# RWKV-6 attention and a SiLU feed-forward block: the recurrent state kept as its diagonal blocks, 48 columns per pair of heads instead of 128

## The chip, the cores and the metric

The kernel runs on one core of a Trainium2 chip. The time is device microseconds of that core, the median of several runs. A profile is one further execution, taken by the hardware profiler; its span runs from the first to the last instruction, and its own time is a little longer than the span.

The engines are named as in the profile: PE is the matrix engine (TensorE), PEld its weight loads, DVE the vector engine, ACT the scalar engine, POOL the GpSimd engine, SP the engine that issues most transfers.

## The reference

Inputs are r, k, v, w of shape (4 batches, 8 heads, 768 tokens, 48), u of shape (8, 48), and two weights of 384x2048 and 2048x384, all float32. Each head of each batch has a 48x48 state:

```python
for t in range(S):
    cur = np.einsum('bhd,bhe->bhde', u[None] * kt, vt)
    y[:, :, t] = np.einsum('bhd,bhde->bhe', rt, state + cur)
    state = wt[:, :, :, None] * state + np.einsum('bhd,bhe->bhde', kt, vt)
x = y.transpose(0, 2, 1, 3).reshape(B * S, H * D)
h = x @ w_in
out = (h * (1.0 / (1.0 + np.exp(-h)))) @ w_out
```

A row of the state belongs to one channel d of the key; the decay w scales a row as a whole.

## The kernel before

**Units.** Time is cut into 6 chunks of 128 tokens, and a unit is one chunk for two batches, so there are 12 units (0 to 11). Inside a unit the decay between tokens is built up in seven levels of doubling distance (`product`, `grow_keys`, `grow_queries`, `score_products`), which fill a 128x128 score per head. `y_state` multiplies the queries with the state of the chunks before (line 844), `y_values` multiplies scores with values (line 865) into the same PSUM banks, and `update` carries the state on. The feed-forward block runs two units behind: `up` (line 1001, then SiLU on ACT, line 1010), and `quarter` (line 1067), which forms the second product by seven products of half size in the manner of Strassen. `sums` makes the sums of activations that these need (DVE, line 1049). The results of the seven products go through two PSUM buffers called `p_o`; `quarter` drains each of them with an addition on DVE (line 1076), or with a copy on ACT for the first (line 1074). A product can start only when the one two places earlier has been drained.

**Pairs of heads.** Two heads share a tile: the even head has partitions 0 to 47, the odd one partitions 64 to 111 (PD = 64, D = 48, NP = 4 pairs). The state has a tile `[128, B, NP, 2 * PD]`, 2048 numbers in each partition. The head e of a pair uses rows 64e to 64e+47 and the columns of the same numbers: a diagonal block. The rest is zero from a memset (line 404) at the start.

**The update of the state** (from line 886). For each of the two batches, PE multiplies keys and values into a PSUM bank `p_kv`, 48 columns for each pair. POOL then multiplies the whole of the batch's state with the decay over the chunk (line 898; not for the units of the first chunk). After the second batch, DVE adds `p_kv` to the diagonal block, one instruction for the even heads and one for the odd heads (line 907). In units 0 and 1 it is a copy, on ACT and on DVE (line 909). Units 10 and 11 have no update, since nothing comes after them.

**The order of the work** is written out by hand: `mix(i)` returns the groups of unit i, and the steps of the feed-forward block are put between them. Each engine runs its own queue in that order. Around the update the order is `turn_apart`, `turn_k`, `y_state(i)`, `y_values(i)`, the transposes of the next unit's w and k on DVE (line 374) with the first `product` on POOL (line 422), a part of `sums`, then `update(i)`. Behind it POOL has `grow_own` (line 654), the other products (line 422) and `grow_own` once more. Unit 2's update stands a little apart: it is followed by unit 3's transposes, the products (line 422) and the start of the keys (line 669). DVE has the additions of `sums`, the addition to the state, the transposes of r (line 374) and `grow_queries` (line 627), and then the first drain of `quarter` (line 1076). `block_bonus` (POOL, line 507) and `block_sum` (DVE, line 541) compute the terms of near tokens.

Of the kernel before, what the change touches and what calls it, by code (L numbers as in the profile page):

```python
# [8 lines left out]
F32 = mybir.dt.float32  # L9
# [29 lines left out]
def kernel(  # L39
# [11 lines left out]
    nc = tc.nc  # L51

    B, H, S, D = r.shape
    DM, DF = moe_w_in.shape
    L = 128
    NL = 7
    NB = 2
    NP = H // 2
    PD = 64
# [14 lines left out]
    const = ctx.enter_context(tc.tile_pool(name="const", bufs=1))  # L74
# [9 lines left out]
    def bank(name, *dims):  # L84

        have = banks[name][turns_of[name] % 2][:]
        turns_of[name] += 1
        steps, n = [], 1
        for d in dims[::-1]:
            steps.insert(0, [n, d])  # L90
            n *= d
        return bass.AP(tensor=have.tensor, offset=have.offset, ap=[have.ap[0], *steps])
# [193 lines left out]
    make_identity(nc, ident)  # L286


    state = const.tile([128, B, NP, 2 * PD], F32, name="state")

    room = pt.tile([128, 4, DM // 2], F32, name="partial", bufs=1).rearrange("p x d -> p (x d)")
    spread = room[:, 0:4 * L].rearrange("p (s b t) -> p s b t", s=2, b=NB)
# [65 lines left out]
    tw, tr, tk, diag, kq, xt = {}, {}, {}, {}, {}, {}  # L358
# [473 lines left out]
    def values(i, b):  # L832
        return vq[i] if b == 1 else vt[i]

    def y_state(i):

        n, b0 = units[i]
        for e in range(2):
            p_yt[i, e] = bank("p_m", NP, L)
        for p in range(NP):  # L840
            for b in range(NB):
                for e in range(2):
                    rows = slice(PD * e, PD * e + D)
                    nc.tensor.matmul(y_place(i, e, p, b), lhsT=state[rows, b0 + b, p, rows],  # L844
                                     rhs=tr[i][rows, b * NP + p, :], start=(p < 2 and b == 0), stop=False)

        half = L // 2
        for p in range(NP):
            for b in range(NB):
                rows, at = slice(b * half, (b + 1) * half), (2 * p + b) * D  # L850
                nc.tensor.matmul(y_place(i, b, p, b)[:, 0:half], lhsT=whole[i][b][rows, at:at + D],
                                 rhs=score[rows, i % NSC, b, b * NP + p, 0:half], start=False, stop=False)

    def y_place(i, e, p, b):

        x = p % 2
        return p_yt[i, e][PD * x:PD * x + D, p // 2 * NB + b, :]
# [27 lines left out]
    def update(i, b):  # L885
        n, b0 = units[i]
        if n == S // L - 1:
            return
        if b == 0:
            p_kv[i] = bank("p_m" if i < NTOK else "p_sc", NB, NP, D)  # L890
        for p in range(NP):
            for e in range(2):
                nc.tensor.matmul(p_kv[i][PD * e:PD * e + D, b, p, :], lhsT=kq[i, b][:, p, PD * e:PD * e + D],
                                 rhs=values(i, b)[:, 2 * p + e, :], start=(b == 0 and p == 0),
                                 stop=(b == NB - 1 and p == NP - 1))
        new = state[:, b0 + b]
        if n > 0:
            nc.gpsimd.tensor_tensor(out=new, in0=new,
                                    in1=tw[i][NL][:, b * NP:(b + 1) * NP, :].to_broadcast([128, NP, 2 * PD]),
                                    op=ALU.mult)  # L900
        if b < NB - 1:
            return
        for e in range(2):
            rows, cols = slice(PD * e, PD * e + D), slice(PD * e, PD * e + D)
            new = state[rows, b0:b0 + NB, :, cols]
            if n > 0:
                nc.vector.tensor_tensor(out=new, in0=p_kv[i][rows], in1=new, op=ALU.add)
            else:
                (nc.scalar.copy if i == 0 else nc.vector.tensor_copy)(out=new, in_=p_kv[i][rows])
# [29 lines left out]
    def mix(i):  # L939
# [15 lines left out]
        def start(j):  # L955
            return [*[(product, j, l) for l in range(1, NL)], (grow_own, j, 1)]

        end = [[*at(ahead, *bonus_steps(i + 1, 0, 1, 2, 3))],
               [*at(i < len(units) - NB, (turn_apart, i), (turn_k, i)), (y_state, i), *both(y_values, i), *at(ahead, *turns(i + 1)),
                (sums, i - 1, FH // 2 - 2), *both(update, i), *at(not ahead, (move_x, i))]]  # L960
        if i < NPAIR:
            groups = [[*both(turn, i, "w"), (product, i, 0)],
# [154 lines left out]
    for l in range(1, NL):  # L1117
# [9 lines left out]


    others = {1: [(bonus_sum, 1, 0), (bonus_sum, 1, 1), (load_rk, 2), *blocks[8:12]], 2: [*both(update, 0)],
              3: [(bonus_spread, 1), (reverse_v, 1), (clear, 1), (load_values, 2)]}  # L1130

# [4 lines left out]
    for m in range(1, 4):  # L1136
# [4 lines left out]
    do((scores, 1, NL - 1), (bonus, 2, 0), (bonus, 2, 1), (join_weight, 8), (add_weight,), (bonus_sum, 2, 0), (bonus, 2, 2), (up, 0, 7), *both(y, 1), (turn_apart, 1),  # L1141
       (tail_weight, 9), (turn_k, 1), (dense_x, 1, 0), (head_weight, 9, [0]), (dense_x, 1, 1), (head_weight, 9, [1]),
       (join_weight, 9), (add_weight,), (tail_weight, 10), (head_weight, 10), *both(update, 1), (bonus_sum, 2, 1), (load_rk, 3), (up, 1, 0), *both(turn, 2, "w"))
    blocks = block_loads(3)

# [5 lines left out]
    for m in range(6):  # L1151
# [8 lines left out]
    do((burst, 2, 5), (keep_level, 2, 5), (keep_level, 2, 6), (go_on, 2, 6), (bonus_write, 2), (up, 1, 6), (weight_sums, 1),  # L1160
       (load_values, 3), (turn_apart, 2), (turn_k, 2), (up, 1, 7), (weight_sums, 2), (sums, 1, 2))
    do((sums, 1, 3), (y_state, 2), *both(y_values, 2), *both(update, 2),
       (move_x, 2),
       *blocks[7:])
# [44 lines left out]
```

## Time and profile before

| what | value |
|---|---|
| median of 3 runs | 600.91 us (600.6 to 602.53) |
| time of the profiled execution | 601.18 us |
| its span | 599.4 us |
| PE busy | 590.6 us, 99% of the span |
| PEld busy | 529.7 us, 88% |
| DVE busy | 417.5 us, 70% |
| POOL busy | 361.3 us, 60% |
| ACT busy | 232.8 us, 39% |
| decay of the state on POOL (line 898) | 16 instructions, 20.7 us |
| memset of the state on POOL (line 404) | 1 instruction, 1.8 us |
| addition to the state on DVE (line 907) | 16 instructions, 8.8 us |
| products with the state on PE (line 844) | 320 matmuls, 48x48 weights, 128 columns |

The shares are means over the whole span. Matmuls overlap, and their ends are modelled, so an idle time of PE that the profile shows is less than the time that the array lost: the spacing of the starts of matmuls is the surer measure. An engine that waits for another is told with the one whose event came last.

### The profile page before, as it was taken

The numbers are of one execution on the slowest core, as the hardware profiler recorded it, in microseconds if no ns is written. First come the engines' busy times: TensorE is split into PE (matmuls) and PEld (weight loads), VectorE is DVE, ScalarE is ACT, GpSimd is POOL, SyncE is SP. The second block draws the span as 40 slices with busy tenths as digits, with TensorE's granted clock in tenths as the row PEclk, the third lists the DMA queues.
The fourth block names the chain that finished last, engine by engine and source line by source line (L and its number), as shares of the span: only waits on it lengthen the run. The fifth ranks groups of instructions, "written<-read, shape, count | busy, mean of one in ns | idle before, by whom it ended". The sixth has DMA issues, their size and how long they took to land.

```text
span 599.4 us, 15465 instructions
## 1 busy us (share of the span) xinstructions
PE 590.6 (99%) x6142; PEld 529.7 (88%) x6142; DVE 417.5 (70%) x709; ACT 232.8 (39%) x516; POOL 361.3 (60%) x414
## 2 busy tenths in 40 slices
PE   8999999999999999999999999999999999999997
PEld 7787876799899899899899889889889889889997
DVE  7879788798696695696696696687588587542041
ACT  6788884431530530540350351361351251250110
POOL 6998778357678568278578478577567567500000
PEclk9999999999999999999999999999999999999999
DMA  9966794342542543642643643643543531101000
GB/s 225 306 143 176 165 277 49 54 80 48 129 61 62 108 68 54 134 63 52 137 63 54 134 61 53 135 61 53 112 77 52 121 57 27 36 2 28 27 1 26
DMA packets 203080, 53.45 MB, mean 89 GB/s; under 512 B 186752, under 2 KB 194816, under 8 KB 203008
## 3 DMA queue, kind: packets, MB, share of 16 engines
q1 hardware_dynamic: 201424, 51.88, 42.3%
q8 instruction: 48, 0.79, 0.6%
q10 hardware_dynamic: 1584, 0.59, 0.5%
q14 instruction: 24, 0.20, 0.1%
HBM read 43.21 MB, written 5.24 MB: 81 GB/s over the span
## 4 chain that ended last, share of the span: by engine, by line
PE 74%; DVE 9%; POOL 4%; DMA 4%; ACT 3%; issue 3%; SPq 3%; DVEq 0%; POOLq 0%; ACTq 0%
PE p_h L1001 31%; PE p_o L1067 31%; PE p_m L1023 3%; PE p_sc L704 2%; PE p_m L865 2%; DVE temps L1049 2%; SPq L123 1%; PE p_m L844 1%; PE p_m L704 1%; DVE score L722 1%; POOL w_in_sb L255 1%; DMA tokens_w<-in_w_dram 1%; POOL tk L645 1%; DVE p_w L242 1%; DMA raw<-in_r_dram 1%
## 5 line engine op out<-in xcount | busy, mean ns | idle before, releaser
L1001 PE MATMUL p_h<-xt,w_in_sb 128*128 128x256 f32 x1152 | 259.5, 382 | 0.8 <-POOL tk L669 0.7
L1001 PEld LDWEIGHTS p_h<-xt,w_in_sb 128*128 128x128 f32 x1152 | 215.6, 190 | 32.1 <-POOL tk L669 0.9
L1010 ACT ACTIVATE gt<-p_h 128x512 f32<-128x512 f32 x90 | 53.5, 596 | 175.4 <-PE p_h L1001 175.1
L645 POOL TENSOR_TENSOR tk<-tk,tw 128x256 f32<-128x256 f32 x128 | 94.6, 759 | 32.9 <-issue 20.8
L1067 PE MATMUL p_o<-own,temps 128*128 128x192 f32 x528 | 88.7, 327 | 0.7 <-DVE temps L1076 0.7
L1067 PEld LDWEIGHTS p_o<-own,temps 128*128 128x128 f32 x528 | 86.0, 190 | 1.6 <-DVE temps L1076 1.6
L507 POOL TENSOR_TENSOR ruk<-tokens_rk 128x768 f32<-128x768 f32 (+1 forms) x32 | 50.6, 1594 | 60.8 <-DMA tokens_rk<-in_k_dram 36.9
L1067 PE MATMUL p_o<-w_out_sb,gt 128*128 128x192 f32 x508 | 86.6, 327 | 0.0
L1067 PEld LDWEIGHTS p_o<-w_out_sb,gt 128*128 128x128 f32 x508 | 83.3, 190 | 1.0 <-DVE partial L1076 0.4
L1049 DVE TENSOR_TENSOR temps<-gt 128x256 f32<-128x256 f32 x84 | 54.9, 653 | 25.5 <-ACT gt L1010 25.3
L627 DVE TENSOR_TENSOR tr<-tr,tw 128x512 f32<-128x512 f32 x61 | 54.8, 899 | 18.3 <-PE p_m L704 14.6
L422 POOL TENSOR_TENSOR tw<-tw 128x256 f32<-128x256 f32 (+6 forms) x83 | 41.0, 494 | 35.8 <-DVE tw L374 31.9
L615 ACT COPY tk<-tk 128x256 f32<-128x256 f32 x52 | 21.0, 403 | 105.2 <-POOL tk L645 77.6
L1049 DVE TENSOR_TENSOR temps<-temps,gt 128x256 f32<-128x256 f32 x43 | 32.6, 759 | 1.5
L722 DVE COPY_PREDICATED score<-mask,p_sc 128x512 f32<-128x512 int8 x42 | 31.2, 799 | 3.5 <-PE p_sc L704 3.3
L1067 PE MATMUL p_o<-w_out_sb,temps 128*128 128x192 f32 x176 | 30.4, 326 | 0.0
L541 DVE TENSOR_REDUCE block_sums<-ruk 128x4 f32<-128x192 f32 (+1 forms) x48 | 24.2, 546 | 7.1 <-POOL ruk L507 7.1
L1067 PEld LDWEIGHTS p_o<-w_out_sb,temps 128*128 128x128 f32 x176 | 28.9, 190 | 0.0
L1076 DVE TENSOR_TENSOR partial<-p_o,partial 128x192 f32<-128x192 f32 x33 | 11.7, 354 | 24.6 <-PE p_o L1067 24.6
L1076 DVE TENSOR_TENSOR temps<-p_o,partial 128x192 f32<-128x192 f32 x22 | 7.9, 358 | 29.8 <-PE p_o L1067 23.5
L870 ACT COPY yt<-p_m 48x512 f32<-48x512 f32 x40 | 23.2, 580 | 13.8 <-PE p_m L865 13.1
L704 PEld LDWEIGHTS p_sc<-tr,tk 48*32 48x32 f32 (+1 forms) x1312 | 18.2, 119 | 11.1 <-issue 8.1
(188 smaller groups left out, 821.9 us busy)
## 6 DMA issues: line engine op xcount, KB each, us to landing
w_out_sb<-in_moe_w_in_dram SPq DMA_DIRECT2D x6, 768.0 KB, 7.5
w_out_sb<-in_moe_w_out_dram SPq DMA_DIRECT2D x4, 768.0 KB, 5.6
own<-in_moe_w_out_dram SPq DMA_DIRECT2D x4, 768.0 KB, 6.4
tokens_rk<-in_r_dram SPq DMA_DIRECT2D x8, 384.0 KB, 4.5
tokens_rk<-in_k_dram SPq DMA_DIRECT2D x8, 384.0 KB, 5.5
tokens_w<-in_w_dram SPq DMA_DIRECT2D x8, 384.0 KB, 6.6
xt<-yt SPq DMA_DIRECT2D x60, 48.0 KB, 2.0
raw<-in_w_dram SPq DMA_DIRECT2D x80, 32.0 KB, 2.0
```

The source lines that it names most:

```text
L422: engine.tensor_tensor(out=up, in0=t[:, :, 0::2], in1=t[:, :, 1::2], op=ALU.mult)
L507: mul = lambda out, one, two: nc.gpsimd.tensor_tensor(out=out, in0=one, in1=two, op=ALU.mult)
L541: add = lambda out, have: nc.vector.tensor_reduce(out=out, in_=have, axis=mybir.AxisListType.X, op=ALU.add)
L627: nc.vector.tensor_tensor(out=odd, in0=odd, in1=tw[i][l][:, :, 0::2][:, :, :, None].to_broadcast([128, Q, L >> (l + 1), c]), op=ALU.mult)
L645: nc.gpsimd.tensor_tensor(out=out, in0=have, in1=odd_products(i, l, b, *blocks), op=ALU.mult)
L704: nc.tensor.matmul(to, lhsT=tk[i][rows, X[l % 2] + p, x * m:(x + 1) * m], rhs=have, start=True, stop=True)
L722: nc.vector.copy_predicated(out=dst, mask=masks[l][:, :, None].to_broadcast([128, NB, NP, ni, c]), data=sc[e].rearrange("p (b q) (i c) -> ...
L870: nc.scalar.copy(out=yt[i][PD * e:PD * e + D, x::2, :, :], in_=p_yt[i, e][PD * x:PD * x + D].rearrange("p (q b) t -> p q b t", b=NB))
L1001: nc.tensor.matmul(p_h[:, a, :], lhsT=w_in_sb[:, c, f * 128:(f + 1) * 128], rhs=xt[i][:, c, :], start=(c == 0), stop=(c == KC - 1))
L1010: nc.scalar.activation(out=gt[i, m], in_=p_h, func=AF.Silu)
L1049: nc.vector.tensor_tensor(out=out, in0=one, in1=two, op=op)
L1067: nc.tensor.matmul(p, lhsT=left(f), rhs=right[:, f, :], start=(f == 0), stop=(f == FH - 1))
```

## The change

The state becomes a tile of 48 columns for each pair of heads. The even head's block and the odd head's block lie in the same columns, on different partitions. The tile has 768 numbers in each partition instead of 2048.

```diff
-    state = const.tile([128, B, NP, 2 * PD], F32, name="state")
+    state = const.tile([128, B, NP, D], F32, name="state")
...
-                    nc.tensor.matmul(y_place(i, e, p, b), lhsT=state[rows, b0 + b, p, rows],
+                    nc.tensor.matmul(y_place(i, e, p, b), lhsT=state[rows, b0 + b, p, :],
                                      rhs=tr[i][rows, b * NP + p, :], start=(p < 2 and b == 0), stop=False)
...
             nc.gpsimd.tensor_tensor(out=new, in0=new,
-                                    in1=tw[i][NL][:, b * NP:(b + 1) * NP, :].to_broadcast([128, NP, 2 * PD]),
+                                    in1=tw[i][NL][:, b * NP:(b + 1) * NP, :].to_broadcast([128, NP, D]),
                                     op=ALU.mult)
...
         for e in range(2):
-            rows, cols = slice(PD * e, PD * e + D), slice(PD * e, PD * e + D)
-            new = state[rows, b0:b0 + NB, :, cols]
+            rows = slice(PD * e, PD * e + D)
+            new = state[rows, b0:b0 + NB]
```

The order of the instructions on every engine and what each waits for stay as they were. The memset on POOL covers 768 numbers a partition instead of 2048, each of the 16 decays on POOL 192 instead of 512, and the additions and copies to the state still cover 384, now in one run instead of 8 runs of 48. The matmuls have the same shapes.

## The prediction

> **What bounds the kernel now.** I read the shares of busy time first, then the stages, then the waits of the engine that is full, then the order of time around one of those waits. From the page:
>
> ```profile
> PE 590.6 (99%) x6142; PEld 529.7 (88%) x6142; DVE 417.5 (70%) x709; ACT 232.8 (39%) x516; POOL 361.3 (60%) x414
> ```
>
> PE is full. The change leaves its 6142 matmuls as they are, so it can win only time in which PE stands still. I cut the span at the starts of the products with the state (line 844), one cut for each unit from 2 on:
>
> ```profile
> core 0: us, PE busy (x) PEld busy (x) DVE busy (x) ACT busy (x) POOL busy (x), PEclk, DMA share, GB/s
> 120.64:166.01 45.37, 45.18 (x549) 41.05 (x549) 37.04 (x57) 15.98 (x39) 29.68 (x33) 1.00 0.46 85
> 166.01:212.85 46.84, 46.53 (x504) 42.39 (x503) 35.53 (x61) 15.40 (x39) 32.28 (x36) 1.00 0.41 76
> 212.85:258.78 45.93, 45.93 (x497) 42.30 (x497) 33.34 (x54) 15.26 (x39) 29.56 (x34) 1.00 0.47 83
> 258.78:305.48 46.70, 46.53 (x504) 42.39 (x504) 35.39 (x60) 15.41 (x39) 31.80 (x36) 1.00 0.46 83
> ...
> 351.47:397.47 46.00, 46.00 (x502) 42.37 (x502) 33.38 (x57) 15.33 (x39) 31.67 (x35) 1.00 0.46 83
> 397.47:443.47 46.00, 46.00 (x502) 42.37 (x502) 33.39 (x56) 15.32 (x39) 30.86 (x35) 1.00 0.43 77
> ```
>
> The second column is the length. Where PE waits for nothing, a stage takes 46.00 us; those after units 3 and 5 take 0.84 and 0.70 us more. The waits of the weight loads from 120 us on say for whom:
>
> ```profile
> PEld p_o L1067 <- DVE temps L1076: 1.6, 3, 0.6
> PEld p_o L1067 <- DVE partial L1076: 0.4, 2, 0.2
> ```
>
> So PE waits for DVE, which drains a PSUM buffer too late. In order of time around one of these waits (start, length, engine, line; times in brackets are idle times):
>
> ```profile
> 263.64 2.50 POOL L898 TENSOR_TENSOR state<-state,tw 128x512 f32<-128x512 f32 x2
> 263.67 0.39 DVE L1049 TENSOR_TENSOR temps<-gt 128x256 f32<-128x256 f32 x1
> ...
> 264.09 1.15 DVE L1049 TENSOR_TENSOR temps<-temps,gt 128x256 f32<-128x256 f32 x1
> ...
> 265.16 1.26 DVE L1049 TENSOR_TENSOR temps<-gt 128x256 f32<-128x256 f32 x1
> 266.10 2.00 POOL L654 TENSOR_TENSOR tk<-tk,tw 128x256 f32<-128x256 f32 x2
> 266.34 1.06 DVE L1049 TENSOR_TENSOR temps<-gt,temps 128x256 f32<-128x256 f32 x1
> ...
> 272.65 0.36 DVE L1076 TENSOR_TENSOR temps<-p_o,partial 128x192 f32<-128x192 f32 x1
> ...
> 273.07 3.19 PE L1067 MATMUL p_o<-own,temps 128*128 128x192 f32 x18 [0.17 <-DVE temps L1076]
> ```
>
> An addition of line 1049 takes 0.39 us when it is alone. Behind each decay of the state on POOL (two of 1.25 us) it takes 1.15 and 1.26 us. DVE has no gap from there to the drain at 272.65. So the two decays delay the drain, and PE with it.
>
> [...] the second addition ends 264.09 + 1.15 = 265.24, some 0.34 us after the first decay's end (263.64 + 1.25 = 264.89); the third ends 266.42, 0.32 us after the second decay. [...] The trace gives 2.13: the POOL multiplications of line 507 over 768 took 1820 ns, of line 448 over 384 1001 ns at best. [...]
>
> **The change part by part.**
>
> *The decays, line 898.* 16 of 512 elements become 16 of 192. For 192 there is a row: 24 multiplications of line 507 at 592 ns. The line through 1001 and 1820 ns gives 182 + 192 x 2.133 = 592 too. So a pair takes 1.18 instead of 2.50 us, and POOL's 20.7 us of busy time become 9.5.
>
> *What DVE gains in a stage.* I walk the rows above again, with the rule that an addition ends 0.33 us after the POOL instruction that held it. Decays end at 264.23 and 264.82, the two of line 654 at 265.82 and 266.82 (their keys, DVE's transposes, end at 263.75, so they can start). The second addition ends 264.56, the third 265.15, the fourth 266.15 instead of 266.34 + 1.06 = 267.40: 1.25 us earlier. Behind it on DVE stand the additions to the state (inputs from PE long done), four more of line 1049, the transposes of r, line 627 and the drain. POOL's next instructions move by 1.32 us, so they meet the same DVE instructions as before. The drain comes at 271.40 instead of 272.65; its product is done at 270.13 + 0.33 = 270.46, so it doesn't wait.
>
> *What PE gains.* From 361 us on, 112 matmuls of line 1067 start in 18.20 us: 0.1625 us each, 2.60 us for a product of 16.
> - After unit 5: the product of 270.13 should be followed at 272.73, and is at 273.07: 0.34. Two products on, the next starts at 278.45 instead of 273.07 + 5.20 = 278.27: 0.18 (the drain at 278.05, behind four reductions of line 541), and the one behind that at 281.16 instead of 281.05: 0.11. With the usual switches this is the 0.70 us of the stage. DVE has to be earlier by at most 0.70 us, and has 1.25.
> - After unit 3 the same places, at 180.44, 185.82 and 188.53: 0.84 us in the stage.
> - After unit 2 the matmuls wait at 132.36 (0.35), at 135.16 for POOL's line 645 (0.11) and at 139.02 (0.10): 0.56 us. There the pair takes 3.26 us, since the first decay waits for DVE's line 1041, and two additions took 1.15 and 1.25 us; the gain is again about 1.2 us.
> - In the other stages PE has no wait to lose: 0. POOL's gain there ends in its next wait, 2.48 us for DVE's line 541.
>
> Sum: 0.84 + 0.70 + 0.56 = 2.10 us.
>
> *The memset, line 404.* From 1806 ns to that of line 303, 737 ns for the same 768: 1.07 us less on POOL at 9.30 us. POOL then waits 2.66 us for DVE's line 422 (to 13.77): 0. Without that cover at most 1.07.
>
> *Additions and copies, lines 907 and 909.* The count per partition stays 384. A copy on DVE of 384 in one run (line 1027) took 557 ns, that to the state in 8 runs 555: 0.
>
> *Products with the state, line 844.* 320 loads at 116 to 120 ns. The new pitch of 48 columns occurs in the values' loads, line 865 (119 to 123 ns), so I take 0. That both halves of the partitions now load from the same columns occurs in line 704, where 32 matmuls take 0.62 us.
>
> *Places in memory.* Tiles behind the state move by 1280 numbers in each partition. Loads of line 1067 take 190 ns from `gt`, `own` and `temps` alike: 0.
>
> The sum against the profiled execution: span 599.4 - 2.1 = 597.3, its time 601.18 - 2.10 = 599.1. The median of the runs, 600.91, is 0.27 lower: 600.91 - 2.10 = 598.8 us.
>
> **The rivals.**
>
> *A. Only a part comes back.* Once PE runs earlier, DVE and POOL must follow. For: what made DVE late in unit 5 is a chain of transfers from 242.9 to 268; if its transfers don't move, PE, already 1.4 us earlier by then, needs 2.1 us of DVE and has 1.25. The transposes of r at 270.24 stand in the chain of work behind a landing of k at 269.67; if that is a true wait, DVE gains 0.6. Against: that chain starts at DVE's line 722 at 237.99, which PE released, so it moves with PE. Between 0.7 (the first waits alone) and 1.7 us: about 599.7 us, no change that can be told.
>
> *B. Nothing comes back.* The 0.4 us lock could be coincidence, and DVE be held elsewhere instead. Against: four additions in a row end a third of a us behind POOL's. 600.9 us.
>
> *C. Slower: the weight loads from the state.* If the even and the odd head's loads from the same columns no longer overlapped, each of the 320 matmuls would take longer than its present 33 ns (32 in 1.06 us); at twice that, 10.6 us more: 598.8 + 10.6 = 609.4. It decides for slower from (1.8 + 2.1) / 320 = 12 ns each. Against: line 704, as above.
>
> *D. More than this.* If the memset's 1.07 us reached the end too: 597.7.
>
> **How the numbers follow.** A difference of 0.3%, 1.8 us, is about what a measurement of this kernel can tell from none; full recovery lies just beyond it, at 599.1 or below. Chances: all of it 0.50, A 0.34, B 0.08, C 0.05, D 0.03. The full case spreads by 0.5 us to each side through the walk and the runs, so about 0.43 of its 0.50 counts as faster; with D 0.46. Its rest, A and B are no change, with 0.01 that B strays above: 0.48. Slower is 0.06. The range leaves out C and the lower half of D: 598.0 to 601.2; the full case alone is 598.3 to 599.3.
>
> **What would show it.** Line 898 at about 0.59 us each; second and third addition of line 1049 at about 0.5 to 0.6 us; the three waits of PE for line 1076 gone; the stages after units 3 and 5 at 46.0 us; line 844 at 1.06 us for 32. The prediction is wrong if the waits stay with the additions shortened, if a wait for another engine takes their place, or if line 844's starts lie further apart.

## The result and the profile after

| what | before | after |
|---|---|---|
| median of the compared runs | 601.24 us (22 runs, 600.6 to 602.76) | 599.96 us (22 runs, 599.15 to 601.49) |
| ratio | | 0.9978, 95% from 0.9972 to 0.9985 |
| decay of the state on POOL (line 898), median | 1266 ns | 734 ns |
| time of the profiled execution, its span | 601.18 us, 599.4 us | 601.36 us, 599.6 us |

The kernel gained 1.3 us of 601 (0.9 to 1.7). That is a gain, since the interval leaves out 1, but it is smaller than the 1.8 us that the prediction took for the least that can be told. The time is 1.15 us above the forecast of 598.8: inside the stated range of 598.0 to 601.2, outside the 598.3 to 599.3 of the case that was given the most chance. The profiled execution after is one of the slowest of its 22 runs, so its span looks like no gain at all. The stages below say why.

The busy shares on the page of the changed kernel, with the number of instructions:

```profile
PE 589.6 (98%) x6142; PEld 529.8 (88%) x6142; DVE 407.8 (68%) x709; ACT 232.8 (39%) x516; POOL 350.9 (59%) x414
```

DVE does the same 709 instructions in 9.7 us less, though the change made none of its instructions smaller, and line 907 takes what it took (551 ns in the median): the additions of line 1049 took 12.5 us less in sum, those of lines 627 and 780 2.7 us more. POOL has 10.4 us less.

The changed lines one by one, on the changed kernel (duration in ns as min/median/max, first and last start in us, forms):

```profile
L898 POOL TENSOR_TENSOR state<-state,tw x16: 678/734/1556, 122.4 to 447.3; 128x192 f32<-128x192 f32 x16
L844 PEld LDWEIGHTS p_m<-tr,state x320: 116/120/120, 121.2 to 534.4; 48*48 48x48 f32 x160
```

The loads from the state cost what they cost before. The decay costs 734 ns and not the 592 of the forecast.

In order of time around the same place of unit 5 as before, the changed kernel (start, length, engine, line):

```profile
263.70 1.43 POOL L898 TENSOR_TENSOR state<-state,tw 128x192 f32<-128x192 f32 x2
263.74 0.38 DVE L1049 TENSOR_TENSOR temps<-gt 128x256 f32<-128x256 f32 x1
264.15 0.61 DVE L1049 TENSOR_TENSOR temps<-temps,gt 128x256 f32<-128x256 f32 x1
264.69 0.72 DVE L1049 TENSOR_TENSOR temps<-gt 128x256 f32<-128x256 f32 x1
265.09 2.00 POOL L654 TENSOR_TENSOR tk<-tk,tw 128x256 f32<-128x256 f32 x2
265.33 1.06 DVE L1049 TENSOR_TENSOR temps<-gt,temps 128x256 f32<-128x256 f32 x1
...
271.63 0.36 DVE L1076 TENSOR_TENSOR temps<-p_o,partial 128x192 f32<-128x192 f32 x1
```

The second and third addition take 0.61 and 0.72 us instead of 1.15 and 1.26. The fourth stands beside line 654 now as then, and takes 1.06 us as before. The drain of line 1076 comes 271.63 - 263.70 = 7.93 us behind the first decay, where it came 272.65 - 263.64 = 9.01 us behind it: 1.08 us earlier, and PE doesn't wait for it any more.

The stages of the changed kernel, cut at the same products (start and end, length, busy times, clock, DMA share, GB/s):

```profile
core 0: us, PE busy (x) PEld busy (x) DVE busy (x) ACT busy (x) POOL busy (x), PEclk, DMA share, GB/s
121.18:165.89 44.71, 44.71 (x549) 41.10 (x549) 36.59 (x59) 15.98 (x39) 27.53 (x32) 1.00 0.45 85
165.89:211.89 46.00, 46.00 (x500) 42.37 (x497) 34.55 (x59) 15.36 (x39) 31.68 (x37) 1.00 0.42 77
211.89:259.56 47.67, 46.24 (x501) 42.29 (x497) 31.96 (x54) 15.45 (x39) 29.10 (x35) 1.00 0.45 82
259.56:305.56 46.00, 46.00 (x500) 42.37 (x497) 33.46 (x61) 15.34 (x39) 29.66 (x35) 1.00 0.46 82
```

Stages 1, 2 and 4 of these (after units 2, 3 and 5) have no wait of PE that shows, and are as short as in any profile here. The one after unit 4, which was at 46.0 before, now takes 47.67. The wait of PE from 118 us on, on the changed kernel (us in total, times, longest), says for what:

```profile
PE p_h L1001 <- DMA xt<-yt: 1.4, 1, 1.4
```

So all waits of PE for DVE are gone, and in this execution most of what they cost has come back in one wait for a transfer. How often that happens is the main question of the experiments.

**A sum that holds for every execution.** In each profile here, the span is 476.7 us, plus the time at which unit 2's first product with the state starts, plus what the four stages behind it have above 44.71, 46.00, 46.00 and 46.00, to within 0.1 us. These four lengths are the shortest in any profile, and I call what lies above them the loss. Before: 476.7 + 120.64 + 2.05 = 599.4. After: 476.7 + 121.18 + 1.67 = 599.55. The start lies between 120.6 and 121.4, in no order that goes with the change (before 120.64, 121.23, 121.30; after 121.18, 120.78, 121.42). No decay has run by then (the first after starts at 122.4 us), so its width can't move the start. A single profile's time therefore can't tell a difference of 1 us; the loss leaves the start out, and says in which stage time goes:

| kernel | start | stages after units 2, 3, 4, 5 | loss |
|---|---|---|---|
| before (first profile) | 120.64 | 45.37, 46.77, 46.00, 46.62 | 2.05 |
| before, again | 121.23 | 45.34, 46.66, 46.22, 46.56 | 2.07 |
| before, third | 121.30 | 45.58, 46.87, 46.05, 46.56 | 2.35 |
| after (first profile) | 121.18 | 44.71, 46.00, 47.67, 46.00 | 1.67 |
| after, again | 120.78 | 44.71, 46.00, 46.00, 46.00 | 0 |
| after, third | 121.42 | 45.20, 46.00, 46.00, 46.00 | 0.49 |
| wide tile, 48 columns used, wide decay | 120.60 | 45.43, 46.51, 46.41, 46.55 | 2.19 |
| wide tile, narrow decay | 121.41 | 44.71, 46.00, 46.92, 46.00 | 0.92 |
| after, `xt` alone sent ahead | 121.07 | 45.49, 46.00, 46.05, 46.00 | 0.83 |
| after, relief of SP | 121.29 | 44.71, 46.00, 46.00, 46.00 | 0 |
| after, relief of SP, again | 121.40 | 44.70, 46.00, 46.00, 46.00 | 0 |
| before, relief of SP | 120.99 | 45.21, 46.39, 46.00, 46.89 | 1.78 |
| after, a memset behind each decay | 121.39 | 44.78, 46.00, 46.04, 46.00 | 0.11 |
| after, a multiplication behind each decay | 121.11 | 45.83, 47.13, 46.04, 47.17 | 3.46 |

(The prediction gives two lengths of the first row as 46.84 and 46.70. Here they are 0.07 and 0.08 shorter, since two of its cuts stood beside the first product; all rows here are cut at the product itself.) The mean loss is 2.16 before and 0.72 after: 1.44 us, against 1.3 measured. With three profiles each, and losses of 0 to 1.67 after, this agreement is a rough one.

### The profile page after: what moved, and what is told of

Read it like the earlier page. It is cut to its first block, busy times and chain, and to the rows that moved or that the text cites. A ratio compares the mean times of both kernels' runs of the same rounds, so it can differ in the third digit from the quotient of the medians.

```text
span 599.6 us, 15465 instructions
## 1 busy us (share of the span) xinstructions
PE 589.6 (98%) x6142; PEld 529.8 (88%) x6142; DVE 407.8 (68%) x709; ACT 232.8 (39%) x516; POOL 350.9 (59%) x414
## 4 chain that ended last, share of the span: by engine, by line
PE 83%; POOL 6%; DVE 4%; ACT 2%; DMA 2%; issue 1%; SPq 1%; DVEq 0%; POOLq 0%; ACTq 0%
PE p_h L1001 38%; PE p_o L1067 31%; PE p_m L1023 3%; PE p_m L865 2%; PE p_sc L704 2%; PE p_m L844 2%; PE p_m L704 2%; POOL tk L645 1%; POOL w_in_sb L255 1%; DMA u_bc<-in_u_dram 1%; PE p_sc L893 1%; PE p_sc L820 1%; POOL w_out_sb L255 1%; DVE score L722 1%; POOL tw L422 1%
## 5 line engine op out<-in xcount | busy, mean ns | idle before, releaser
L645 POOL TENSOR_TENSOR tk<-tk,tw 128x256 f32<-128x256 f32 x128 | 92.7, 745 | 42.2 <-issue 24.3
L1049 DVE TENSOR_TENSOR temps<-gt 128x256 f32<-128x256 f32 x84 | 48.6, 579 | 26.9 <-ACT gt L1010 26.8
L654 POOL TENSOR_TENSOR tk<-tk,tw 128x256 f32<-128x256 f32 x32 | 27.6, 883 | 0.0
```

The costliest lines, as they stand in the source:

```text
L645: nc.gpsimd.tensor_tensor(out=out, in0=have, in1=odd_products(i, l, b, *blocks), op=ALU.mult)
L654: nc.gpsimd.tensor_tensor(out=have, in0=have, in1=odd_products(i, l, b, [2, NP * ni]), op=ALU.mult)
L1049: nc.vector.tensor_tensor(out=out, in0=one, in1=two, op=op)
```

## The experiments

**The two kernels again.** Of the changed kernel, twice:

> The changed kernel once more, for a second trace of it. Theory 1: the narrower decay on POOL frees DVE earlier, and PE's waits for line 1076 are gone: the stages after units 2, 3 and 5 at 44.7, 46.0 and 46.0 us again (45.37, 46.84 and 46.70 before). Theory 2: a part of that gain, 1.43 us in the first trace, is taken back in the stage after unit 4, where PE waits for the transfers of xt: that stage at 46.5 to 47.7 us here too. Rival of theory 2: one late transfer by accident, and the stage takes 46.0 us now. Time against before: 1.0 to 1.6 us less.

> The changed kernel on the same chip as the two before and the one behind. Stages after units 2, 3 and 5 at 44.7, 46.0 and 46.0 us; in the stage after unit 4 a wait for xt between 0 and 1.7 us. 1.0 to 1.6 us less than before.

Measured: 600.21 us (9 runs), ratio 0.9978 (0.9968 to 0.9987), and 600.36 us (4 runs), 0.9974 (0.9960 to 0.9988). The kernel before, twice more:

> The kernel before once more, for a second trace: the stages after units 2, 3 and 5 longer by 0.4 to 0.9 us each than without a wait (44.7, 46.0 and 46.0), the one after unit 4 at 46.0, and the start of unit 2's product with the state at 120.6 to 121.0 us. If instead its waits are small here, the mean gain to be had is below the forecast 2.1 us.

> The same once more, with the same expectation. The two together tell whether the later start seen with narrow decays, 120.8 to 121.4 us against 120.6 to 121.0 with wide ones, is chance: if it is, these starts spread up to 121.4 too.

Measured: 601.78 and 601.80 us (2 runs each), ratios 0.9999 and 1.0000, both with an interval of about 0.998 to 1.0018. What follows: the gain of 1.3 us repeats, and the starts of before spread up to 121.30, so a late start doesn't belong to the narrow decays. The wait of 1.43 us for `xt` is not in every execution: the stage after unit 4 takes 46.00 us in both new profiles of the changed kernel, where I had expected 46.5 to 47.7 of the first of them. The third profile of the changed kernel waits at another place, in unit 3. In its order of time (SPq is SP's queue of DMA issues; idle times with their releaser in brackets):

```profile
152.66 2.44 SPq L467 DMA_DIRECT2D diag<-own_sums  x4
155.06 0.20 ACT L595 COPY both_b<-diag 128x16 f32<-128x16 f32 x1 [1.75 <-DMA diag<-own_sums]
...
163.21 2.46 PEld L1001 LDWEIGHTS p_h<-xt,w_in_sb 128*128 128x128 f32 x12 [0.49 <-ACT gt L1010]
```

In the second profile of the same kernel, which has no loss, the same issues stand 1.5 us earlier (0.86 us earlier if counted from the start of unit 2), and ACT waits 0.88 us for them instead of 1.75:

```profile
151.16 2.45 SPq L467 DMA_DIRECT2D diag<-own_sums  x4
```

ACT waits for `diag`, so its SiLU (line 1010) comes late, and PE waits for that. Both places, `xt` in unit 4 and `diag` in unit 3, hang on when SP's queue gets to an issue.

**Which part of the change.** One kernel keeps the 48 columns in a tile of 128 and decays all 128 of them: the reads, the additions and the loads are those of the changed kernel, the width of the decay and the memset are those of before.

```diff
-    state = const.tile([128, B, NP, D], F32, name="state")
+    state = const.tile([128, B, NP, 2 * PD], F32, name="state")
...
-                    nc.tensor.matmul(y_place(i, e, p, b), lhsT=state[rows, b0 + b, p, :],
+                    nc.tensor.matmul(y_place(i, e, p, b), lhsT=state[rows, b0 + b, p, 0:D],
...
-                                    in1=tw[i][NL][:, b * NP:(b + 1) * NP, :].to_broadcast([128, NP, D]),
+                                    in1=tw[i][NL][:, b * NP:(b + 1) * NP, :].to_broadcast([128, NP, 2 * PD]),
...
-            new = state[rows, b0:b0 + NB]
+            new = state[rows, b0:b0 + NB, :, 0:D]
```

> Both heads' blocks in columns 0 to 47 as in the changed kernel, but the tile keeps 128 columns for a pair (the same memset of 2048 numbers, the same places of the tiles behind it) and POOL's decay covers all 512 elements. Theory 1 (the width of the decay is the cause): like before, 601.2 us, the stages after units 3 and 5 at 46.8 and 46.7 us, two additions of line 1049 at 1.15 and 1.25 us. Rival (the new columns, or the additions in fewer runs, are the cause): like the changed kernel, 600.0 us, those stages at 46.0.

Measured: 601.39 us (13 runs), ratio 0.9998 (0.9990 to 1.0007): nothing of the gain. In order of time around the same decays:

```profile
263.77 2.50 POOL L898 TENSOR_TENSOR state<-state,tw 128x512 f32<-128x512 f32 x2
...
264.22 1.15 DVE L1049 TENSOR_TENSOR temps<-temps,gt 128x256 f32<-128x256 f32 x1
...
265.29 1.26 DVE L1049 TENSOR_TENSOR temps<-gt 128x256 f32<-128x256 f32 x1
```

The additions are as long as before, to the hundredth. The other kernel has the same wide tile, and only the decay is narrowed (shown against the changed kernel; the lines on the tile, the loads and the additions are those above):

```diff
-        new = state[:, b0 + b]
+        new = state[:, b0 + b, :, 0:D]
         if n > 0:
             nc.gpsimd.tensor_tensor(out=new, in0=new,
                                     in1=tw[i][NL][:, b * NP:(b + 1) * NP, :].to_broadcast([128, NP, D]),
```

> As the one before, but POOL's decay covers 48 of the 128 columns of each pair. The memset and the places in memory stay those of before. Theory 1: like the changed kernel, 1.0 to 1.6 us less than before, the stages after units 3 and 5 at 46.0 us. Rival (the smaller memset or the places in memory bring the gain): like before, 601.2 us.

Measured: 599.93 us (21 runs), ratio 0.9975 (0.9969 to 0.9982): all of the gain. What follows: the width of the 16 decays is the whole of the change. The memset, the 1280 numbers of each partition that the tile gives up or not, the additions in one run or in eight and the columns of the loads make no difference that shows.

**What holds DVE.** Narrow decays make POOL earlier as well as DVE. Two kernels on top of the changed one tell these apart. The first fills the time that POOL won with a memset of as many numbers as the decay had:

```diff
+    idle = const.tile([128, NP, 2 * PD], F32, name="idle")
...
         nc.gpsimd.memset(state, 0.0)
+        nc.gpsimd.memset(idle, 0.0)
...
                                     op=ALU.mult)
+            nc.gpsimd.memset(idle, 0.0)
```

> The changed kernel with a memset of 512 numbers a partition on POOL behind each decay, on a tile that nothing reads: POOL is as late as before (0.72 + 0.52 us for each decay instead of 1.25), but in the added time it reads nothing from SBUF. Theory 1a (DVE waits [...]): like the changed kernel, within 0.5 us; the second and third addition of line 1049 at about 0.6 to 0.7 us. Theory 1b (DVE and PE are late because POOL's later work is late): like before, 601.3 us, the stages after units 3 and 5 at 46.7 us or more.

Measured: 599.92 us (6 runs), ratio 0.9971 (0.9959 to 0.9982). In its order of time (its lines lie 2 or 3 further down: 900 is the decay, 903 the memset, 1052 the addition, 656 the keys):

```profile
263.09 0.79 POOL L900 TENSOR_TENSOR state<-state,tw 128x192 f32<-128x192 f32 x1
263.54 0.62 DVE L1052 TENSOR_TENSOR temps<-temps,gt 128x256 f32<-128x256 f32 x1
263.82 0.52 POOL L903 MEMSET idle<- 128x512 f32 x1
264.08 0.41 DVE L1052 TENSOR_TENSOR temps<-gt 128x256 f32<-128x256 f32 x1
264.31 0.56 POOL L900 TENSOR_TENSOR state<-state,tw 128x192 f32<-128x192 f32 x1
...
265.29 1.64 POOL L656 TENSOR_TENSOR tk<-tk,tw 128x256 f32<-128x256 f32 x2
```

POOL gets to the keys 2.20 us behind the first decay, nearly as late as before (266.10 - 263.64 = 2.46), and later than in the changed kernel (1.39). The time is that of the changed kernel. The addition that starts during the memset takes 0.41 us, about the median of such additions before (425 ns). The second kernel has a multiplication in place of the memset, with two inputs in SBUF like the decay:

```diff
+            nc.gpsimd.tensor_tensor(out=idle, in0=idle,
+                                    in1=tw[i][NL][:, b * NP:(b + 1) * NP, :].to_broadcast([128, NP, 2 * PD]),
+                                    op=ALU.mult)
```

> The changed kernel with a further multiplication of 512 elements on POOL behind each decay, on a tile of zeros that nothing else reads: a pair of decays takes 2 x (0.72 + 1.25) = 3.94 us instead of 2.50 before. Theory 1: DVE is some 1.4 us later than in the kernel before in each stage. PE, which had about 1.4 us to spare in the stages after units 4 and 6 to 9, waits little there; after units 2, 3 and 5 it waits 1.2 to 1.4 us more each. Sum 3.5 to 5 us more than before: 604.5 to 606.5 us. If the width of the decay is not what holds DVE: 601.3 us or less.

Measured: 603.37 us (7 runs), ratio 1.0026 (1.0014 to 1.0037). In its order of time (903 is the added multiplication, 1054 the addition of `sums`, 912 the one to the state, 1081 the drain):

```profile
264.90 0.79 POOL L900 TENSOR_TENSOR state<-state,tw 128x192 f32<-128x192 f32 x1
265.65 1.21 POOL L903 TENSOR_TENSOR idle<-idle,tw 128x512 f32<-128x512 f32 x1
265.89 1.25 DVE L1054 TENSOR_TENSOR temps<-gt 128x256 f32<-128x256 f32 x1
...
267.48 1.21 POOL L903 TENSOR_TENSOR idle<-idle,tw 128x512 f32<-128x512 f32 x1
267.71 1.11 DVE L912 TENSOR_TENSOR state<-p_sc,state 48x384 f32<-48x384 f32 x2
...
274.38 0.36 DVE L1081 TENSOR_TENSOR temps<-p_o,partial 128x192 f32<-128x192 f32 x1
```

The same addition takes 1.25 us beside the multiplication and 0.41 beside the memset. The multiplication is longer than the memset (1.21 us against 0.52), so these two kernels alone don't compare equal POOL time; the kernel with the memset and the one before do, nearly, and differ by the whole gain. So POOL's lateness is not what costs: 2.20 us to the keys with the memset and 2.46 before stand beside 599.92 and 601.24 us. What costs here is POOL's multiplication of two tiles in SBUF beside DVE's addition of two tiles there (1.25 us, against that median of 425 ns). Not every addition beside a decay is held: unit 5's first one starts 0.03 us behind the first decay before and 0.04 after (263.67, 263.74) and takes 0.39 and 0.38 us, so the prediction's 0.39 is not that of an addition alone. By what means the one holds the other, no run here shows.

The size that I gave for this kernel was too large. The drain comes 274.38 - 264.90 = 9.48 us behind the first decay, only 0.47 later than before. The second added multiplication stands beside the additions to the state, whose one input is in PSUM, and these took 1.11 us for two, as in the profile before (541 to 561 ns each). So part of the added POOL time held nobody. The loss of 3.46 is 1.3 above the mean of before, and the time 1.6 us above (0.8 to 2.2).

**Where the rest of the gain went.** The first profile of the changed kernel around its one wait (SPq as above):

```profile
227.89 2.91 SPq L123 DMA_DIRECT2D raw<-in_k_dram  x6
...
230.91 6.28 SPq L929 DMA_DIRECT2D xt<-yt  x10
...
237.43 1.13 PE L1001 MATMUL p_h<-xt,w_in_sb 128*128 128x256 f32 x4
...
239.99 2.18 PE L1001 MATMUL p_h<-xt,w_in_sb 128*128 128x256 f32 x9 [1.43 <-DMA xt<-yt]
```

SP's queue issues the loads of a later unit's keys ahead of the ten transfers of `xt`, which PE is about to read. PE starts at 237.43, does four matmuls, and stands still for 1.43 us until 239.99. The last two of the ten transfers (durations of an issue in ns, then us from issue to landing):

```profile
L929 SPq DMA_DIRECT2D xt<-yt x2: 589/590/591, 236.0 to 236.6; - x2
DMA to landing us min/median/max: 2.0/2.6/3.3
```

One of the two landed 3.3 us after its issue. In six other profiles (before, after again and third, the wide tile with the narrow decay, `xt` alone sent ahead, the relief of SP again), each landing of these ten that the trace has came within 2.0 us. So some 1.3 of the 1.67 us that this stage lost are one slow transfer, and about 0.4 the late issue (an estimate: 3.3 - 2.0, and the rest). The order of the issues costs time without a slow transfer too: the wide tile with narrow decays lost 0.92 at the same place, where PE waits 0.7 us for `xt`. And a kernel with wide decays meets it as well: the wide tile with the wide decay lost 0.41 in that stage, where PE waits 0.2 us for `xt`.

I first held back the last four loads of that one unit (twelve transfers), so that `xt` comes first:

```diff
+    held = []
     def mix(i):
...
+        groups[1] += held * (i == NPAIR + 1)
...
-            group += loads[at * len(loads) // len(behind):(at + 1) * len(loads) // len(behind)]
+            (held if i == NPAIR and at == len(behind) - 1 else group).extend(loads[at * len(loads) // len(behind):(at + 1) * len(loads) // len(behind)])
```

> The changed kernel with one move in SP's queue, after unit 4: the ten transfers of xt are issued ahead of the last twelve loads of k for unit 6 (some 5.9 us earlier) instead of behind them. Theory 2 (PE, being earlier, now meets those transfers): the stage after unit 4 at 46.0 us, and 0.7 to 1.4 us less than the changed kernel, 598.6 to 599.3 us. Rival (that wait was an accident of one execution): the same as the changed kernel within 0.3 us, 599.7 to 600.2.

Measured: 600.17 us (8 runs), ratio 0.9977 (0.9964 to 0.9990). The wait for `xt` is gone (the `xt` issues start at 224.85, the stage takes 46.05), but the time is not lower, as the rival in the expectation had it. In that profile 0.78 us go to the other place, in unit 3, where ACT waits 2.01 us for `diag` and PE three times for ACT's line 1010. So both places were relieved: the last group of loads of each unit goes behind the transfers that the next unit's up product and `diag` need.

```diff
+    held = {i: [] for i in range(len(units) + 1)}
     def mix(i):
...
+        groups[9 if i < NPAIR else 1] += held[i]
...
-            group += loads[at * len(loads) // len(behind):(at + 1) * len(loads) // len(behind)]
+            (held[i + 1] if at == len(behind) - 1 and i + NSLOT < len(units) else group).extend(loads[at * len(loads) // len(behind):(at + 1) * len(loads) // len(behind)])
...
-       *blocks[7:])
-
+       *blocks[7:10])
+    held[3] = blocks[10:]
```

> The changed kernel with SP's queue put in another order: the last twelve loads of k in each unit from 3 to 9 stand behind the transfers of xt instead of ahead of them, and the last eight loads of r for unit 4 behind the four transfers of diag in unit 3. Theory 2 (with DVE earlier, PE next meets SP's queue, in unit 3 through diag and in unit 4 through xt): 0.4 to 0.9 us less than the changed kernel, 599.1 to 599.6 us, and the stages after units 2, 3, 4 and 5 at 44.7, 46.0, 46.0 and 46.0 us. Rival (what is missing of the forecast 2.1 us lies elsewhere, in the start or in the runs of before): as the changed kernel, 599.9 to 600.2 us.

> The changed kernel with SP's queue in the other order, now beside the changed kernel on one chip. If PE's waits for xt and diag are what takes back a part of the gain: no wait of PE from 121 us on and 0.4 to 0.7 us less than the changed kernel. If they are rare: the same within 0.3 us.

Measured: 599.76 us (5 runs), ratio 0.9963 (0.9950 to 0.9975), and 599.72 us (4 runs), 0.9964 (0.9949 to 0.9978). Both profiles have a loss of 0: each of the four stages has its shortest length, as expected, though the first time is a little above the expected 599.1 to 599.6. The order of time of the second one at `xt`:

```profile
225.52 6.28 SPq L929 DMA_DIRECT2D xt<-yt  x10
231.85 6.01 SPq L123 DMA_DIRECT2D raw<-in_k_dram  x12
...
237.64 4.58 PE L1001 MATMUL p_h<-xt,w_in_sb 128*128 128x256 f32 x20
```

`xt` is issued 5.4 us earlier than in the first profile of the changed kernel, the key loads behind it, and PE starts at 237.64 without a break. The same edit on the kernel before:

> The same reordering of SP's queue on the kernel before. Theory 2: PE waits for DVE there and the transfers are in time, so nothing or little is gained: 600.9 to 601.4 us, against 601.3. Rival (SP's queue costs time whatever POOL does): 0.4 to 0.9 us less than before.

Measured: 601.13 us (20 runs), ratio 0.9988 (0.9981 to 0.9996). So SP costs the kernel before something as well: 0.7 us (0.2 to 1.1). I had expected nothing or little; the rival in the expectation fits better. Its profile has a loss of 1.78, and in these stages PE and its weight loads wait for other engines only at DVE's line 1076 (2.4 us in 7 waits) and, 0.8 us in sum, for POOL.

The four times together, against before: the relief alone -0.7 us, the narrow decay alone -1.3 (0.9 to 1.7), both -2.2 (1.5 to 3.0 in the one comparison, 1.3 to 3.1 in the other). Within these intervals the two gains simply add. With the relief in both, the narrow decays bring 1.4 us by the medians (601.13 to 599.76, and the ranges don't overlap): hardly more than the 1.3 without it.

The kernel with both has the lowest medians of those that ran. Beside the changed kernel on the same chip it took 599.72 us against 600.36 (4 runs each, and their ranges overlap: 598.94 to 600.20 and 599.99 to 600.39).

## Why the prediction was right or wrong

- **What bounds the kernel, and for whom PE waits: right in the main.** The narrow decay alone has the whole gain, the wide one none. (One wait of the weight loads, for ACT, was left out; see rival A.) With narrow decays no wait for line 1076 is left in any profile but that of the added multiplication (its line 1081: 1.9 us in 3 waits of PE), and the stages after units 3 and 5 stand at 46.00 in all three profiles of the changed kernel.
- **The decay at 592 ns: too low.** It takes 734 ns in the median, and a pair 1.43 us instead of 1.18. I took the time of a row of the same size (line 507). Here DVE's additions run beside it. In units 3 to 9 of the kernel with the memset, the first decay takes 0.79 us each time, and the second, behind the memset, 0.55 to 0.56. What makes the first longer, no run here isolates.
- **DVE 1.25 us earlier: 1.08.** The second decay ends 1.43 us behind the start of the first instead of 1.18, and so does everything behind it; the fourth addition ends 2.69 us behind that start, where I had 2.51 and before had 3.76. The prediction's third of a microsecond is 0.27 and 0.28 us here: the first decay takes 0.79 us and ends at 264.49, the second addition ends at 264.76; the second decay ends at 265.13, the third addition at 265.41. It was 0.28 before, too: that first decay took 1.32 us, not the 1.25 of the mean, and ended at 264.96, the addition at 265.24. PE needed 0.70 at most, so the difference had no effect.
- **PE's gain of 0.84 + 0.70 + 0.56 = 2.10 us: the waits were there and went, but the sum is too large.** This is the step that failed: the narrow decays brought 1.3 us, and 1.4 with the transfers relieved in both kernels. Three things are known. First, the stages after units 3 and 5 stood 0.77 and 0.62 us above 46.00, not 0.84 and 0.70, so the sum is 1.95; the three waits listed for unit 5 make 0.63 by themselves, and there were no "usual switches" to add. Second, the sum took the stage after unit 4 (46.0 in that one profile) as one with no wait to lose, and the shortest length of the other stages as reachable; but transfers on SP's queue took 1.67, 0 and 0.49 us in these stages in the three profiles of the changed kernel, 0.72 in the mean, some 0.4 of it through the one slow landing. Before, they took an estimated 0.1 to 0.4 of the 2.16 (DVE's waits make up nearly all of the 2.05 of the first profile, and of the 1.78 in the profile with the relief). Third, a gain read from one profile is uncertain by some tenths: the same three stages of before lose 1.85 to 2.3 us. When those transfers are issued earlier, no loss is left and 2.2 us are won, but 0.7 of these the relief brings without the narrow decays. How the missing 0.8 us divide among these, the runs don't settle.
- **Rival A: right in size, wrong in its place.** It said that a transfer which doesn't move with PE would take back part, a gain of 0.7 to 1.7 us, and gave 599.7, nearer to the measured 599.96 than my forecast. But its place was the chain from 242.9 to 268 us, through DVE. That chain gave way: the transposes of r start 5.52 us behind the first decay instead of 6.60. What held in the profiles was `xt` on PE itself, at 240 us, and `diag` through ACT. Of `xt` the profile that I read shows no wait. Of `diag` it shows something: ACT waited 1.38 us for it, and then the weight loads for ACT's line 1010. I left this line out of the waits that I listed:

```profile
PEld p_h L1001 <- ACT gt L1010: 0.3, 1, 0.3
```

- **Rival B**, nothing: excluded (ratio below 0.9985). **Rival C**, slower weight loads: excluded, 116 to 120 ns for line 844 as before. **Rival D**, the memset: it went from 1806 to 744 ns and nothing came of it, since the wide tile with its old memset is as fast as the changed kernel.
- **The base.** 600.91 was the median of 3 runs; of 22 it is 601.24. This is 0.33 of the 1.15 us by which the forecast time is too low; the other 0.82 is the gain of 1.28 instead of 2.10. That the time still lies in the stated range is the width of that range, which took rival A in; it doesn't confirm the sum.

What stays open: whether PE meets SP's queue *because* it is earlier. The mean loss to transfers (0.1 to 0.4 before, 0.72 after) suggests it, but without the one slow landing the second is about 0.3, the kernel with wide decays waits for `xt` too, and the times of the four combinations add up without it. Three profiles of each kernel don't settle a difference of this size. Also open is why unit 2 starts anywhere from 120.6 to 121.4 us: the mean is 120.95 over the five profiles with wide decays and 121.23 over the nine with narrow ones, though nothing that the width of the decay changes has run by then.

## What to carry to other kernels

Of an engine that is off the bound, ask what it blocks, not how busy it is: here POOL was busy for 60% of the span, and cutting its decays from 1266 to 734 ns cut DVE's additions beside them from 1.15 and 1.26 us to 0.61 and 0.72. When a wait of the full engine goes, look for the next thing that comes only a little ahead of need: here transfers issued behind loads that nobody needs yet, for which PE then waited 1.43 us in one profile. Where one execution shows a long wait for a transfer, look whether that transfer was issued late or was slow (here one landed after 3.3 us, where six other profiles had 2.0 at most). And take a gain that is the sum of three waits from more than one profile, at the stages and not at the span, when starts scatter by 0.8 us and the gain is 1.3.

## What I had not expected of the hardware

- Two kinds of POOL work beside an addition on DVE differed: beside a multiplication of 512 the addition took 1.25 us, beside a memset of 512 0.41.
- A memset of 512 numbers on POOL took 0.52 us, a multiplication of 512 1.21.
- The transfers of `xt` in unit 4 took 1.8 to 2.0 us from issue to landing in six profiles, and up to 3.3 in the one in which PE waited 1.43 us for them.
